# Long convolution plus top-128 experts: another order of GpSimd's work at the column loops, and another layout of the buffers there

## The chip, the cores and the metric

The kernel runs on one core of a Trainium2 chip. TensorE (PE in the profile), VectorE (DVE), ScalarE (ACT) and GpSimd (POOL) each run their own instruction list in order and meet at semaphores. SyncE (SP) issues nearly all DMAs, in order as well. The metric is device microseconds of one execution, the median of several; it is compared with the kernel before on the same chip.

## The reference

For 4 sequences of 12608 rows and 128 channels, in float32:

```
h_filt = (relu(pos_emb @ w1) @ w2) * exp(-0.01 * pos)
y = irfft(rfft(x * v, 2S) * rfft(h_filt, 2S), 2S)[:S]      # causal long convolution
x = x * y
# per sequence: the 128 rows with the highest score x @ w_gate get
out[row] = x[row] + sigmoid(score) * (relu(x[row] @ moe_w1) @ moe_w2)
```

All other rows of the output are x * y.

## The kernel before

The transforms are small matrix products. A sequence is laid out as a 111 x 115 grid, and the channels are worked in 32 groups of 4. There are 128 group steps t (4 sequences of 32), software-pipelined: step t does the inverse product of group t-3 (`f_i`, its result copied by ACT into `big`), the forward second product of group t (`dft`), the first product of group t+1 (`f_s1`), on DVE the spectrum product (`f_m`, `f_y`) of group t-1, on POOL the sums and differences of that spectrum (`f_sd` of t-1) and the product x * v for the input of group t+3 (`stage_u`). So POOL gets four operations a step, two of `f_sd` (L423, L424) and two of `stage_u` (L218, L219).

After the last group of a sequence, inside step 34, 66, 98 or 130, stands the column loop `P1.run` (L514). It finishes 116 columns in 29 turns h of four columns. Eight columns, two turns, make a block; there are 15 blocks. In a turn PE does the last small product (`mm`, L479 and L474), DVE multiplies it with x in place (`fin`, L489) and with the gate weights (L508), ACT sums the scores (L510), and after every second turn SP stores the block (L501) and loads x for the block five further on (L450). A load into a buffer waits until the store from that buffer has landed.

For blocks 2 to 14 POOL prepares, for four of the eight columns, the sum and the difference of two column planes (`comb`, L462); PE then needs half of the products for those columns and reads them at L474. Three such pairs of buffers are rotated (`cm`), and `comb` of three blocks is issued ahead of the loop.

At the three loops that are not the last, step 34 (66, 98) also completes the spectrum of its own group at once: line 959 runs `f_m`, `f_y` and `f_sd` of group 34 ahead of the loop, since the pipeline would otherwise hold the buffers through the loop.

All buffers are slices of one SBUF tile `arena`. Two of the six x buffers of the loop (XE) and the third `cm` pair (CE) are not slices of their own but lie over buffers of the group steps: `qs`, `mt`, `yz` and, behind these, `ws`, the scratch of the top-128 search. In words per partition these lie at: te 0, qs 1776, mt 2664, yz 3552 (two of 888), ws 5328 (640). CE is 1776 to 2800, the two XE 2800 to 3824 and 3824 to 4848. The loads into XE (blocks 4 and 5, issued ahead of the loop) therefore wait for all work on `mt` and `yz`. What may wait for what is worked out by the framework from these overlaps; the order on each engine is the order of the code.

Of the kernel before, what the change touches and what calls it, by code (L numbers as in the profile page):

```python
# [17 lines left out]
B, S, D, FO = 4, 12608, 128, 64  # L18
# [5 lines left out]
NG = 32  # L24
HC = 4 * N1
# [11 lines left out]
LAG = 3  # L37
# [4 lines left out]
NC, CO = 4, 2  # L42
# [5 lines left out]
CB = range(2, (NJ + 7) // 8)  # L48
PC = 4
OFF, _o = {}, 0  # L50
for _n, _k, _w in (("te", 2, 2 * HC), ("qs", 2, HC), ("mt", 1, 2 * HC), ("yz", 2, 2 * HC), ("ws", 1, 640), ("sd", LAG, 2 * HC),
                   ("ht", NH, 2 * HC), ("xa", NX, 8 * D), ("wx", 2, HB * D), ("cm", 2, 2 * NC * D), ("u", NU, 2 * XC)):
    OFF[_n] = (_o, _k, _w)
    _o += _k * _w
ARENA = _o
CE = OFF["qs"][0]
XE = [CE + 2 * NC * D + k * 8 * D for k in range(2)]
POS0, HID0 = 0, PJ * N1


# [80 lines left out]
def hyena_moe(ctx, tc, xg, x2, pos, bw, ww, wg, mw1, mw2, fo, c1, gx, cf, ci, wm, tk, zr, out):  # L141
    nc = tc.nc
# [6 lines left out]
    arena = cp.tile([128, ARENA], F32, name="arena")  # L149
    big = cp.tile([128, D * 2 * NJ], F32, name="big")  # L150

    def view(t, off, shape):
        n = int(np.prod(shape[1:]))
        r = t[:shape[0], off:off + n]
        if len(shape) > 2:
            ax = "abcd"[:len(shape) - 1]
            r = r.rearrange(f"p ({' '.join(ax)}) -> p {' '.join(ax)}", **dict(zip(ax[1:], shape[2:])))
        return r

    def buf(name, k, shape):  # L160
        o, n, w = OFF[name]
        return view(arena, o + k % n * w, shape)
# [40 lines left out]
    def rev(t):  # L203
        return t.rearrange("p (s i) -> p s i", i=N1)[:, :, ::-1]

    def nat(t):
        return t.rearrange("p (s i) -> p s i", i=N1)
# [6 lines left out]
    def stage_u(t):  # L214
        if t >= B * NG:
            return
        u = buf("u", t, [N1, 2, XC])
        nc.gpsimd.tensor_tensor(out=u[:, 0], in0=u[:, 0], in1=u[:, 1], op=ALU.mult)  # L218
        nc.gpsimd.tensor_tensor(out=u[:, 1].rearrange("p (s j) -> p s j", s=4),  # L219
                                in0=u[:, 0].rearrange("p (s j) -> p s j", s=4), in1=sg, op=ALU.mult)  # L220
# [186 lines left out]
    def f_m(t, uv):  # L407
        ht = buf("ht", t, [128, 2, HC])
        mt = buf("mt", t, [128, 2, HC])
        nc.vector.tensor_tensor(out=mt, in0=uv, in1=ht[:, 0].unsqueeze(1).to_broadcast([128, 2, HC]), op=ALU.mult)  # L410
        nc.vector.tensor_tensor(out=uv, in0=uv, in1=ht[:, 1].unsqueeze(1).to_broadcast([128, 2, HC]), op=ALU.mult)  # L411
        return mt

    def f_y(t, uv, mt):
        yz = buf("yz", t, [128, 2, HC])
        nc.vector.tensor_tensor(out=yz[:, 0], in0=uv[:, 1], in1=mt[:, 0], op=ALU.add)
        nc.vector.tensor_tensor(out=yz[:, 1], in0=mt[:, 1], in1=uv[:, 0], op=ALU.subtract)  # L417
        return yz

    def f_sd(t, yz):  # L420
        sd = buf("sd", t, [128, 2, HC])
        eng = nc.vector if t == B * NG - 1 else nc.gpsimd
        eng.tensor_tensor(out=nat(sd[:, 0]), in0=nat(yz[:, 0]), in1=rev(yz[:, 1]), op=ALU.add)  # L423
        eng.tensor_tensor(out=nat(sd[:, 1]), in0=rev(yz[:, 0]), in1=nat(yz[:, 1]), op=ALU.subtract)  # L424
        return sd.rearrange("p e (s i) -> p e s i", i=N1)
# [11 lines left out]
    class P1:  # L437
# [6 lines left out]
        def load_a(self, k):  # L444
            if k < len(blocks):
                j0, j1 = blocks[k]
                o = k % (NX + len(XE))
                self.xa[k] = buf("xa", o, [128, 8, D]) if o < NX else view(arena, XE[o - NX], [128, 8, D])
                for t in range(2):
                    nc.sync.dma_start(self.xa[k][t * NQ:t * NQ + PR, :j1 - j0], x2[self.b, t * PR:(t + 1) * PR, j0:j1])  # L450

        def comb(self, k):
            if k not in CB:
                return
            j0, j1 = blocks[k]
            j0 += CO
            n = min(NC, j1 - j0)
            o = (k - CB[0]) % 3
            cm = buf("cm", o, [128, 2, NC, D]) if o < 2 else view(arena, CE, [128, 2, NC, D])
            av = [ay[:, :, e * NJ + j0:e * NJ + j0 + n].rearrange("p g j s -> p j g s") for e in range(2)]  # L460
            for e, op in enumerate((ALU.add, ALU.subtract)):
                nc.gpsimd.tensor_tensor(out=cm[:, e, :n].rearrange("p j (g s) -> p j g s", s=4), in0=av[0], in1=av[1],  # L462
                                        op=op)
            self.cm[k] = cm

        def mm(self, h):
            ja, n = hbs[h]
            ps = self.s4[h] = ps1(h % 3, [128, HB, D], f"s4_{self.b}_{h}")
            for k in range(n - 1, -1, -1) if ja % 8 else range(n):
                j = ja + k  # L470
                a, c = CSH * j % N1, CSH * (N2 - j) % N1
                if j // 8 in CB and CO <= j % 8 < CO + NC:
                    for t, o in enumerate((a, c)):
                        nc.tensor.matmul(ps[t * NQ:(t + 1) * NQ, k], lhsT=gx_sb[:, o:o + NQ],  # L474
                                         rhs=self.cm[j // 8][:, t, j % 8 - CO], start=True, stop=True)
                    continue
                for e in range(2):
                    for t, o in enumerate((a, c + e * GW)):
                        nc.tensor.matmul(ps[t * NQ:(t + 1) * NQ, k], lhsT=gx_sb[:, o:o + NQ], rhs=ay[:, :, e * NJ + j],  # L479
                                         start=e == 0, stop=e == 1)  # L480

        def fin(self, h):
# [15 lines left out]
            if ja + n == blocks[blk][1]:  # L498
# [3 lines left out]
                if blk:  # L502
                    self.load_a(blk - 1 + NX + len(XE))

# [9 lines left out]
        def run(self, ex):  # L514
            self.wg = ps2(1, [128, D], f"wg_{self.b}")
            nc.scalar.copy(out=self.wg, in_=wgb)
            for k in range(len(XE)):
                self.load_a(NX + k)
            for k in range(3):
                self.comb(CB[0] + k)  # L520
            for h in range(len(hbs)):
                self.mm(h)
                self.fin(h)
                if h % 2 and h // 2 >= CB[0]:
                    self.comb(h // 2 + 3)
                if ex:
                    ex.hook(h, self.wg)
            nc.vector.tensor_tensor(out=self.sc, in0=self.sc, in1=negm, op=ALU.min)
            return self.sc
# [384 lines left out]
        nc.vector.memset(t, 0.0)  # L914
    h_hid()
    h_spec()
    te, uv, mt, sd, ph = {}, {}, {}, {}, {}
    bg = Background(iter(()))
    te[0] = f_s1(0)
    NT = B * NG  # L920
    for t in range(NT + LAG):
        g = t % NG
        i = t - LAG
        if 0 <= i:
            f_i(i, sd.pop(i))
        if t < NT:
            pq = ps2(1 - t % 2, [128, 2, 512], f"pq_{t}")
            spare[0] = [a[:, 512 - NS:] for a in bank1]
            uv[t] = pq[:, :, :HC]
            bg.now = t  # L930
            qs = dft(t, te.pop(t), (uv[t][:, 0], uv[t][:, 1]))
            bg.hook("p", 1)
            bg.hook("n", 1)
            if t + 1 < NT:
                te[t + 1] = f_s1(t + 1)
            spare[0] = None
            bg.hook("w", 1)
            load_u(t + NU - 1)
            if t == 8:
                for r in (PR, NQ + PR):  # L940
                    nc.sync.dma_start(arena[r:r + NQ - PR, OFF["xa"][0]:OFF["xa"][0] + NX * 8 * D], zr)
            o = t - 1 in uv
            if o:
                m = f_m(t - 1, uv[t - 1])
            f_v(uv[t], qs)
            for _ in range(ND):
                bg.hook("d")
            if o:
                y = f_y(t - 1, uv.pop(t - 1), m)
            f_u(uv[t], qs)  # L950
            if o:
                sd[t - 1] = f_sd(t - 1, y)
            stage_u(t + 3)
            if t:
                load_h(t + 2)
            for _ in range(NE):
                bg.hook("e")
            if i >= 0 and i % NG == NG - 1 or t == NT - 1:
                sd[t] = f_sd(t, f_y(t, uv[t], f_m(t, uv.pop(t))))
        if t >= NT:  # L960
            bg.now = t
            for _ in range((3, 1, 0)[t - NT]):
                bg.hook("p")
                for _ in range(ND):
                    bg.hook("d")
            bg.hook("w", 1)
        b = i // NG
        if i >= 0 and i % NG in LA:
            if i % NG == LA[0]:
                ph[b] = P1(b)  # L970
            ph[b].load_a(LA.index(i % NG))
        if i % NG == NG - 1 and i >= 0:
            bg.drain()
            ex = Experts(picked) if b + 1 == B else None
            sc = ph.pop(b).run(ex)
            bg = Background(topk_one(b, sc, ex))
# [50 lines left out]
```

## Time and profile before

| | us |
|---|---|
| median of 3 runs | 944.06 (943.54 to 945.16) |
| profiled execution, its own time | 944.23 |
| its span in the trace | 942.3 |
| PE busy | 902.8 (96%) |
| DVE busy | 854.4 (91%) |
| POOL busy | 769.3 (82%) |
| ACT busy | 613.3 (65%) |

PE's granted clock is 0.995 of full over the span. The span is the time from the first to the last instruction; 1.9 us of the execution's own time lie outside it. An engine's busy share is an average over three kinds of stretch: the filter's spectrum at the start, the group steps, and the column loops. The loops start at about 279, 473, 667 and 855 us of the span.

### The profile page before, as it was taken

What the parts mean: (1) busy time and instruction counts of PE and PEld (TensorE: products, weight loads), DVE (VectorE), ACT (ScalarE), POOL (GpSimd) and SP (SyncE); (2) the same over time, 40 slices, a digit from 0 to 9 for tenths busy, and PEclk for the clock granted to TensorE, in tenths of its full rate; (3) what the DMA queues carried; (4) which work ended last, traced back from release to release, by engine and by line L of the source; (5) the groups of instructions that cost most, each with busy time, mean ns of one, the idle gap of its engine ahead of it and who ended that gap; (6) DMA issues with size and microseconds to landing.
All of it is one profiled execution on the core that took longest, in us unless ns stands there. A gap on an engine that the chain in (4) does not pass through costs nothing.

```text
span 942.3 us, 37826 instructions
## 1 busy us (share of the span) xinstructions
PE 902.8 (96%) x15518; PEld 831.1 (88%) x15518; DVE 854.4 (91%) x1570; ACT 613.3 (65%) x1983; POOL 769.3 (82%) x714
## 2 busy tenths in 40 slices
PE   8999999999999999999999999999999999998964
PEld 5877789999999899999999999999999999988953
DVE  7999999999998899999988999999899999997974
ACT  5655545555547887865568878755599878545920
POOL 4898859999999579999998599999994999986701
PEclk9999999999999999999999999999999999999998
DMA  8144497666876886667958966669589666655830
GB/s 238 60 176 177 177 267 194 204 195 194 228 209 199 294 230 195 186 189 198 252 163 290 243 191 191 192 185 250 169 289 267 200 192 189 185 145 151 273 120 9
DMA packets 61408, 187.39 MB, mean 199 GB/s; under 512 B 8757, under 2 KB 12708, under 8 KB 61220
## 3 DMA queue, kind: packets, MB, share of 16 engines
q1 hardware_dynamic: 60980, 184.45, 65.1%
q8 instruction: 123, 2.02, 0.9%
q0 software_dynamic: 256, 0.52, 0.2%
q14 instruction: 49, 0.40, 0.1%
HBM read 143.52 MB, written 41.42 MB: 196 GB/s over the span
## 4 chain that ended last, share of the span: by engine, by line
PE 79%; DVE 6%; POOL 5%; DMA 4%; ACT 3%; issue 3%; SPq 0%; POOLq 0%; ACTq 0%; DVEq 0%
PE c L246 18%; PE c L230 10%; PE c L229 10%; PE a L230 10%; PE a L229 9%; PE a L479 5%; PE c L382 3%; PE a L362 3%; PE c L362 3%; PE c L479 3%; PE a L474 2%; ACT arena L510 2%; DMA out_dram<-arena 1%; POOL arena L423 1%; POOL arena L424 1%
## 5 line engine op out<-in xcount | busy, mean ns | idle before, releaser
L229 PE MATMUL c<-ci_sb,arena 128*56 128x116 f32 x2048 | 224.8, 263 | 4.3 <-POOL arena L423 2.0
L230 PE MATMUL c<-ci_sb,arena 128*55 128x116 f32 x2048 | 224.9, 263 | 0.0
L246 PE MATMUL c<-arena,cf_sb 128*64 128x222 f32 x2048 | 217.6, 351 | 2.2 <-DVE arena L417 1.9
L229 PE MATMUL a<-c_sb,arena 111*58 111x111 f32 x2048 | 217.0, 259 | 0.0
L230 PE MATMUL a<-c_sb,arena 111*57 111x111 f32 x2048 | 216.8, 259 | 0.0
L229 PEld LDWEIGHTS c<-ci_sb,arena 128*56 128x56 f32 x2048 | 206.5, 130 | 5.9 <-POOL arena L423 2.2
L230 PEld LDWEIGHTS c<-ci_sb,arena 128*55 128x55 f32 x2048 | 206.4, 129 | 0.0
L229 PEld LDWEIGHTS a<-c_sb,arena 111*58 111x58 f32 x2048 | 199.2, 132 | 4.3 <-issue 0.3
L230 PEld LDWEIGHTS a<-c_sb,arena 111*57 111x57 f32 x2048 | 199.0, 131 | 2.9
L423 POOL TENSOR_TENSOR arena<-arena 128x444 f32<-128x444 f32 x127 | 133.7, 1053 | 82.6 <-DVE arena L417 77.6
L246 PEld LDWEIGHTS c<-arena,cf_sb 128*64 128x64 f32 x2048 | 154.1, 137 | 27.6 <-ACT arena L238 2.3
L238 ACT COPY arena<-a 128x444 f32<-128x444 f32 x256 | 135.3, 530 | 63.6 <-PE a L230 63.2
L432 ACT COPY big<-c 128x928 f32<-128x928 f32 x128 | 118.3, 924 | 78.1 <-PE c L230 74.4
L510 ACT ACTIVATE arena<-arena 128x128 f32<-128x128 f32 x448 | 133.0, 298 | 27.4 <-DVE arena L508 25.2
L218 POOL TENSOR_TENSOR arena<-arena 111x460 f32<-111x460 f32 x128 | 150.2, 1174 | 0.0
L219 POOL TENSOR_TENSOR arena<-arena,wm_sb 111x460 f32<-111x460 f32 x128 | 139.4, 1089 | 10.0
L410 DVE TENSOR_TENSOR arena<-c,arena 128x888 f32<-128x888 f32 x128 | 138.4, 1081 | 3.8
L411 DVE TENSOR_TENSOR c<-c,arena 128x888 f32<-128x888 f32 x128 | 138.3, 1080 | 0.0
L424 POOL TENSOR_TENSOR arena<-arena 128x444 f32<-128x444 f32 x127 | 134.6, 1060 | 0.0
L462 POOL TENSOR_TENSOR arena<-big 128x512 f32<-128x512 f32 (+1 forms) x104 | 125.1, 1262 | 8.9 <-ACT big L432 5.6
L249 ACT COPY arena<-c 128x444 f32<-128x444 f32 x128 | 67.8, 529 | 58.6 <-PE c L246 55.2
L479 PE MATMUL a<-big,gx_sb 128*64 128x128 f32 x1472 | 100.6, 273 | 3.0 <-DVE arena L489 1.9
(188 smaller groups left out, 1675.8 us busy)
## 6 DMA issues: line engine op xcount, KB each, us to landing
arena<-hd SPq DMA_DIRECT2D x128, 444.0 KB
arena<-in_xg_dram SPq DMA_DIRECT2D x128, 402.5 KB
arena<-in_x_dram SPq DMA_DIRECT2D x112, 224.0 KB
out_dram<-arena SPq DMA_DIRECT2D x112, 224.0 KB
hd<-arena SPq DMA_DIRECT2D x32, 444.0 KB
arena<-in_pos_dram SPq DMA_DIRECT2D x14, 222.0 KB
arena<-in_moe_w_dram SPq DMA_DIRECT2D x2, 512.0 KB
arena<-in_x_dram SPq DMA_DIRECT2D x8, 112.0 KB
```

Of the source, the lines that this page charges most:

```text
L218: nc.gpsimd.tensor_tensor(out=u[:, 0], in0=u[:, 0], in1=u[:, 1], op=ALU.mult)
L219: nc.gpsimd.tensor_tensor(out=u[:, 1].rearrange("p (s j) -> p s j", s=4), in0=u[:, 0].rearrange("p (s j) -> p s j", s=4), in1=sg, op=ALU.mult)
L229: nc.tensor.matmul(o[:h], lhsT=lhsT[:, :h], rhs=rhs, **kw)
L230: nc.tensor.matmul(o[NQ:NQ + m - h], lhsT=lhsT[:, h:], rhs=rhs, **kw)
L238: nc.scalar.copy(out=te[:, e], in_=tps[e])
L246: nc.tensor.matmul(pq[w][e * NQ:(e + 1) * NQ, c], lhsT=cf_sb[:, 2 * w + e], rhs=te[:, e, c], start=True, stop=True)
L410: nc.vector.tensor_tensor(out=mt, in0=uv, in1=ht[:, 0].unsqueeze(1).to_broadcast([128, 2, HC]), op=ALU.mult)
L411: nc.vector.tensor_tensor(out=uv, in0=uv, in1=ht[:, 1].unsqueeze(1).to_broadcast([128, 2, HC]), op=ALU.mult)
L423: eng.tensor_tensor(out=nat(sd[:, 0]), in0=nat(yz[:, 0]), in1=rev(yz[:, 1]), op=ALU.add)
L424: eng.tensor_tensor(out=nat(sd[:, 1]), in0=rev(yz[:, 0]), in1=nat(yz[:, 1]), op=ALU.subtract)
L479: nc.tensor.matmul(ps[t * NQ:(t + 1) * NQ, k], lhsT=gx_sb[:, o:o + NQ], rhs=ay[:, :, e * NJ + j], start=e == 0, stop=e == 1)
L510: nc.scalar.activation(out=wx[:, k], in_=wx[:, k], func=AF.Copy, accum_out=self.sc[:, ja + k:ja + k + 1])
```

## The change

Three things move, and nothing is added or taken away in the count of operations.

At the loops inside steps 34, 66 and 98 `f_sd` of the step's own group is no longer issued ahead of the loop. `f_y` still is; its result stays in `yz` (`ys`), and `f_sd` runs one step later, where the ordinary pipeline has it. `stage_u` of group 37 (69, 101) is no longer issued ahead of the loop either, but in turn 23, behind the last `comb`.

The buffers are laid anew: the first XE lies at 1776 to 2800 (qs and the head of mt), the second at 4440 to 5464 (the second yz and the head of ws), and the two halves of the third `cm` pair at 2800 to 3312 (mt) and 5464 to 5976 (ws, which grows by 8 words). The first yz, which holds `ys` through the loop, is left free.

```
-XE = [CE + 2 * NC * D + k * 8 * D for k in range(2)]
+XE = [CE, OFF["yz"][0] + 2 * HC]
+CE = [XE[0] + 8 * D, XE[1] + 8 * D]
...
+                if h // 2 == CB[-1] - 3 and h % 2:
+                    stage_u((self.b + 1) * NG + 5)
...
-            if o:
-                sd[t - 1] = f_sd(t - 1, y)
-            stage_u(t + 3)
+            if o or t - 1 in ys:
+                sd[t - 1] = f_sd(t - 1, y if o else ys.pop(t - 1))
+            if i < 0 or i % NG < NG - 1:
+                stage_u(t + 3)
...
             if i >= 0 and i % NG == NG - 1 or t == NT - 1:
-                sd[t] = f_sd(t, f_y(t, uv[t], f_m(t, uv.pop(t))))
+                ys[t] = f_y(t, uv[t], f_m(t, uv.pop(t)))
+            if t == NT - 1:
+                sd[t] = f_sd(t, ys.pop(t))
```

In the rows of the order below, a bracket names the semaphores that an instruction waits for: an engine's, or one of the eight lanes DMAHW0 to DMAHW7 on which SP's DMAs land in turn. From `f_y` on the changed file's lines are one to four higher: `stage_u` is L219 and L220, `f_sd` L424 and L425, `comb` L464.

POOL at the first loop, from behind `f_sd` of group 33. Before:

```order
L218 TENSOR_TENSOR arena<-arena 111x460 [waits DMAHW3_49]
L219 TENSOR_TENSOR arena<-arena,wm_sb 111x460 [waits Pool_49]
L423 TENSOR_TENSOR arena<-arena 128x444 [waits DVE_49,PE_49]
L424 TENSOR_TENSOR arena<-arena 128x444 [waits PE_49]
L462 TENSOR_TENSOR arena<-big 128x512 [waits Activation_49]
L462 TENSOR_TENSOR arena<-big 128x512 x3
L462 TENSOR_TENSOR arena<-big 128x512 [waits Activation_49]
L462 TENSOR_TENSOR arena<-big 128x512
L462 TENSOR_TENSOR arena<-big 128x512 [waits PE_49,Pool_49] x18
L462 TENSOR_TENSOR arena<-big 128x256 [waits PE_49,Pool_49] x2
```

The same place on POOL in the changed kernel:

```order
L464 TENSOR_TENSOR arena<-big 128x512 [waits Activation_49]
L464 TENSOR_TENSOR arena<-big 128x512 x3
L464 TENSOR_TENSOR arena<-big 128x512 [waits DVE_49]
L464 TENSOR_TENSOR arena<-big 128x512
L464 TENSOR_TENSOR arena<-big 128x512 [waits PE_49,Pool_49] x18
L464 TENSOR_TENSOR arena<-big 128x256 [waits PE_49,Pool_49] x2
L219 TENSOR_TENSOR arena<-arena 111x460 [waits DMAHW3_49]
L220 TENSOR_TENSOR arena<-arena,wm_sb 111x460 [waits Pool_49]
L424 TENSOR_TENSOR arena<-arena 128x444
L425 TENSOR_TENSOR arena<-arena 128x444
```

The 26 `comb` operations now stand ahead of the four others, and the third pair waits for DVE.

SP at the same loop: the last load of a filter spectrum (`hd`), the four DMAs into the two XE (`in_x_dram`), and the stores of blocks 0 and 1. Before:

```order
L224 DMA arena<-hd 128x888 [waits DMAHW6_49,DVE_49]
L450 DMA arena<-in_x_dram 56x1024 [waits DMAHW7_49,DVE_49,Pool_49]
L450 DMA arena<-in_x_dram 56x1024 [waits DMAHW0_49]
L450 DMA arena<-in_x_dram 56x1024 [waits DMAHW1_49]
L450 DMA arena<-in_x_dram 56x1024 [waits DMAHW2_49]
L501 DMA out_dram<-arena 56x1024 [waits DMAHW3_49,DVE_49]
```

The same place on SP in the changed kernel:

```order
L225 DMA arena<-hd 128x888 [waits DMAHW6_49,DVE_49]
L451 DMA arena<-in_x_dram 56x1024 [waits DMAHW7_49,DVE_49,Activation_49]
L451 DMA arena<-in_x_dram 56x1024 [waits DMAHW0_49]
L451 DMA arena<-in_x_dram 56x1024 [waits DMAHW1_49,Pool_49]
L451 DMA arena<-in_x_dram 56x1024 [waits DMAHW2_49]
L503 DMA out_dram<-arena 56x1024 [waits DMAHW3_49,DVE_49]
```

The DMAs keep their order. The first load no longer waits for POOL; the third does. In the built program the values waited for name the instructions: before, DVE's L417 and POOL's L424 of group 34; in the changed kernel DVE's first operation of `f_y` of group 34 (L416 in the lines of before) and ACT's copy of `qs` of group 34 for the first load, and POOL's L424 of group 33 for the third.

DVE at the end of the first loop: the mask of the scores, then the start of the top-128 search, and the first operation of the next group step. Before:

```order
L528 TENSOR_TENSOR sc_2948<-sc_2948,tk_sb 128x116 [waits DVE_49,Activation_49]
L575 TENSOR_SCALAR f_4084<-sc_2948 128x116 [waits DVE_49]
L577 TENSOR_TENSOR sc_2948<-sc_2948,f_4084 128x116 [waits DVE_49]
L578 COPY hi_4085<-sc_2948 128x116 [waits DVE_49]
L650 CAST arena<-sc_2948 128x116
L405 TENSOR_TENSOR c_72<-c_72,arena 128x444 [waits Activation_49,Pool_49]
```

The same place on DVE in the changed kernel:

```order
L532 TENSOR_TENSOR sc_2948<-sc_2948,tk_sb 128x116 [waits DVE_49,Activation_49]
L579 TENSOR_SCALAR f_4082<-sc_2948 128x116 [waits DVE_49]
L581 TENSOR_TENSOR sc_2948<-sc_2948,f_4082 128x116 [waits DVE_49]
L582 COPY hi_4083<-sc_2948 128x116 [waits DVE_49]
L654 CAST arena<-sc_2948 128x116 [waits DMAHW4_49,DMAHW3_49]
L406 TENSOR_TENSOR c_72<-c_72,arena 128x444 [waits Activation_49]
```

The cast writes the head of `ws`, which now lies under the second XE, so it waits for the two lanes of the store of block 11, the last block in that buffer.

## Rows read from the trace of the kernel before

**Rows 1.** Groups by line: count | busy us, mean ns | idle before, by releaser.

```profile
L229 PE MATMUL c<-ci_sb,arena 128*56 128x116 f32 x2048 | 224.8, 263 | 4.3 <-POOL arena L423 2.0 <-DVE arena L423 0.8 <-ACT big L432 0.7
```

**Rows 2.** The waits: who waited for whom, us in total, times, longest.

```profile
PE a L474 <- POOL arena L462: 3.8, 6, 0.8
```

**Rows 3.** Timeline of PE, loop 1: start, us, engine, line, operation, count [idle before].

```profile
287.91 0.43 PE L474 MATMUL a<-arena,gx_sb 128*64 128x128 f32 x2 [0.42 <-POOL arena L462]
...
293.45 1.03 PE L479 MATMUL c<-big,gx_sb 128*64 128x128 f32 x14
...
297.38 1.03 PE L479 MATMUL c<-big,gx_sb 128*64 128x128 f32 x14
...
317.02 1.09 PE L479 MATMUL a<-big,gx_sb 128*64 128x128 f32 x16 [0.79 <-DVE arena L489]
...
322.33 0.26 PE L229 MATMUL c<-ci_sb,arena 128*56 128x116 f32 x1
```

**Rows 4.** Timeline of POOL, loop 1 and behind it.

```profile
282.27 1.16 POOL L218 TENSOR_TENSOR arena<-arena 111x460 f32<-111x460 f32 x1
...
285.57 1.06 POOL L424 TENSOR_TENSOR arena<-arena 128x444 f32<-128x444 f32 x1
286.58 31.21 POOL L462 TENSOR_TENSOR arena<-big 128x512 f32<-128x512 f32 x26
...
333.81 1.05 POOL L423 TENSOR_TENSOR arena<-arena 128x444 f32<-128x444 f32 x1 [13.73 <-DVE arena L417]
```

**Rows 5.** Timeline of SP's queue, loop 1: us is the time of issuing.

```profile
286.65 2.13 SPq L450 DMA_DIRECT2D arena<-in_x_dram  x4
288.89 3.15 SPq L501 DMA_DIRECT2D out_dram<-arena  x4
...
295.72 1.47 SPq L501 DMA_DIRECT2D out_dram<-arena  x2
...
320.57 7.86 SPq L501 DMA_DIRECT2D out_dram<-arena  x10
```

**Rows 6.** The waits of SP's queue, 275 to 300 us.

```profile
SPq L450 <- POOL arena L424: 2.6, 1, 2.6
```

**Rows 7.** Timeline of DVE, loop 1.

```profile
282.85 0.62 DVE L416 TENSOR_TENSOR arena<-c,arena 128x444 f32<-128x444 f32 x1
...
291.13 0.69 DVE L489 TENSOR_TENSOR arena<-c,arena 128x512 f32<-128x512 f32 x1
...
307.16 0.69 DVE L489 TENSOR_TENSOR arena<-a,arena 128x512 f32<-128x512 f32 x1 [1.64 <-DMA arena<-in_x_dram]
...
327.94 0.21 DVE L650 CAST arena<-sc 128x116 f32<-128x116 uint16 x1
```

**Rows 8.** Windows: busy by engine, then granted clock, DMA share, GB/s.

```profile
280.00:285.00 5.00, 5.00 (x92) 4.79 (x90) 4.86 (x8) 0.27 (x1) 4.68 (x5) 1.00 0.15 60
...
305.00:310.00 5.00, 5.00 (x94) 4.98 (x92) 3.32 (x6) 3.32 (x23) 5.00 (x5) 1.00 0.90 297
```

**Rows 9.** Timeline of PE, loops 2 and 3: first L474, first product behind the loop.

```profile
482.24 0.43 PE L474 MATMUL a<-arena,gx_sb 128*64 128x128 f32 x2 [0.57 <-POOL arena L462]
...
516.75 0.26 PE L229 MATMUL c<-ci_sb,arena 128*56 128x116 f32 x1
...
676.09 0.43 PE L474 MATMUL a<-arena,gx_sb 128*64 128x128 f32 x2 [0.43 <-POOL arena L462]
...
709.43 0.26 PE L229 MATMUL c<-ci_sb,arena 128*56 128x116 f32 x1
```

**Rows 10.** Timeline of DVE, loops 2 and 3: first operation of f_y.

```profile
477.04 0.62 DVE L416 TENSOR_TENSOR arena<-c,arena 128x444 f32<-128x444 f32 x1
...
671.02 0.62 DVE L416 TENSOR_TENSOR arena<-c,arena 128x444 f32<-128x444 f32 x1
```

**Rows 11.** Timeline of SP's queue, loops 2 and 3: the loads into XE.

```profile
481.00 1.84 SPq L450 DMA_DIRECT2D arena<-in_x_dram  x4
...
674.84 1.60 SPq L450 DMA_DIRECT2D arena<-in_x_dram  x4
```

More of the change, by code (lines that the diff above doesn't have):

```diff
@@ L50 @@
 OFF, _o = {}, 0
-for _n, _k, _w in (("te", 2, 2 * HC), ("qs", 2, HC), ("mt", 1, 2 * HC), ("yz", 2, 2 * HC), ("ws", 1, 640), ("sd", LAG, 2 * HC),
+for _n, _k, _w in (("te", 2, 2 * HC), ("qs", 2, HC), ("mt", 1, 2 * HC), ("yz", 2, 2 * HC), ("ws", 1, 648), ("sd", LAG, 2 * HC),
                    ("ht", NH, 2 * HC), ("xa", NX, 8 * D), ("wx", 2, HB * D), ("cm", 2, 2 * NC * D), ("u", NU, 2 * XC)):
@@ L458, in comb @@
             o = (k - CB[0]) % 3
-            cm = buf("cm", o, [128, 2, NC, D]) if o < 2 else view(arena, CE, [128, 2, NC, D])
+            cm = buf("cm", o, [128, 2, NC, D]) if o < 2 else None
+            cm = [view(arena, c, [128, NC, D]) if cm is None else cm[:, e] for e, c in enumerate(CE)]
             av = [ay[:, :, e * NJ + j0:e * NJ + j0 + n].rearrange("p g j s -> p j g s") for e in range(2)]
             for e, op in enumerate((ALU.add, ALU.subtract)):
-                nc.gpsimd.tensor_tensor(out=cm[:, e, :n].rearrange("p j (g s) -> p j g s", s=4), in0=av[0], in1=av[1],
+                nc.gpsimd.tensor_tensor(out=cm[e][:, :n].rearrange("p j (g s) -> p j g s", s=4), in0=av[0], in1=av[1],
                                         op=op)
@@ L474, in mm @@
                         nc.tensor.matmul(ps[t * NQ:(t + 1) * NQ, k], lhsT=gx_sb[:, o:o + NQ],
-                                         rhs=self.cm[j // 8][:, t, j % 8 - CO], start=True, stop=True)
+                                         rhs=self.cm[j // 8][t][:, j % 8 - CO], start=True, stop=True)
                     continue
@@ L916, in hyena_moe @@
     h_spec()
-    te, uv, mt, sd, ph = {}, {}, {}, {}, {}
+    te, uv, ys, sd, ph = {}, {}, {}, {}, {}
     bg = Background(iter(()))
```

## The prediction

> **What bounds the kernel now.** I read the page first: PE is busy for 902.8 of 942.3 us, so only its gaps can be won, and a slower engine matters where PE waits for it. The groups by line give PE's gaps at the step's products: a few us in all, 0.7 of them behind ACT's copy (L432), which stands just behind the column loops [rows 1]. The list of waits then names the gap that the change speaks of: PE at L474 waits for POOL's `comb`, six times, 3.8 us [rows 2]. Six is two in each of three loops; the fourth loop has none.
>
> The timelines of loop 1, one engine at a time, show why. PE comes to L474 at 287.49 (287.91 less 0.42 idle) [rows 3]. POOL starts its 26 `comb` operations only at 286.58, since it first runs `stage_u` of group 37 from 282.27 and `f_sd` of group 34 to 286.63 [rows 4]. That is the visible stall.
>
> The second thing stands on SP's queue. The loads of x for blocks 4 and 5 go out at 286.65 [rows 5], 0.02 us after POOL's L424 ends, and the queue's own waits say so: 2.6 us for that POOL operation, once [rows 6]. Everything behind them in the queue is late as well: the store of block 2 goes out at 295.72 [rows 5], though DVE finished turn 5, the block's last, at 291.82 (291.13 + 0.69) [rows 7]. In the window 280 to 285 the DMA engines are busy for 0.15 of the time, in 305 to 310 for 0.90 [rows 8]: the loop's DMA stream starts late and then runs close to full. DVE pays for it: at 307.16 it has been idle 1.64 us for x [rows 7], the first and longest of four such waits in loop 1 (3.75 us in all); and through DVE's result PE pays again, 0.79 us at 317.02 [rows 3].
>
> So in these loops two chains lie side by side, PE's products and SP's stream of x, and the later one sets the end.
>
> **The change part by part.** *The comb moved ahead.* POOL can start `comb` at 282.27 instead of 286.58 [rows 4]. The first pair (two operations; 31.21 us / 26 = 1.20 each) is ready by about 284.8, 2.7 us before PE's 287.49. The third pair waits for `f_y`, whose first operation ends at 283.47 [rows 7] and whose second follows directly (about 284.0); POOL reaches that pair at about 287. So PE's 3.8 us of stall go. Taken alone that is worth little: DVE would only arrive sooner at loads that come no sooner.
>
> *The new layout.* The first load then waits for the first operation of `f_y` (end 283.47, plus the 0.02 us of before: 283.49) and ACT's copy of `qs`, long done; the third for `f_sd` of group 33, done when POOL starts `stage_u` at 282.27. The stream of loop 1 starts 286.65 - 283.49 = 3.16 us earlier. In loops 2 and 3 `f_y`'s first operation ends at 477.66 and 671.64 [rows 10] and the loads go out at 481.00 and 674.84 [rows 11]: 3.32 and 3.18 us. The trace doesn't show how much of such a lead reaches the loop's end. From above it is all of it; from below nothing more than DVE's own lead, 1.2 us a loop, if stores wait for results. I take all of it, because the store of block 2 stands 3.9 us behind its result (295.72 against 291.82), more than the lead: the queue, not the result, is late from the start.
>
> *What PE can take.* Turns 8 and 11 start 293.45 and 297.38 [rows 3]: 3.93 us for three turns of 24 recorded products, 0.0546 us each. Behind the first L474 wait stand 25 turns less the 16 records of two full columns, 584 x 0.0546 = 31.89 us, less 0.22 because 287.49 is the end of a product and not its issue: 31.67. Measured from there to the first product behind the loop: 322.33 - 287.49 = 34.84 [rows 3]; 516.75 - 481.67 = 35.08 and 709.43 - 675.66 = 33.77 [rows 9]. PE's slack is thus 3.17, 3.41 and 2.10 us, POOL's stall included.
>
> *The smaller of lead and slack* is what a loop gives: 3.16 (loop 1), 3.32 (loop 2), 2.10 (loop 3), in sum 8.6 us. Behind the loops the group steps are PE-bound, so the lead stays. The waits for ACT's copy behind the loops, 0.7 us in all [rows 1], may shrink in loop 3; I count nothing.
>
> *The steps moved back.* `stage_u` of 37 and `f_sd` of 34 (1.05 to 1.16 us each by their rows, two and two) now run behind the last `comb`, with `stage_u` of 38 behind them: some 4.3 us more than POOL has there before. POOL is idle there for 13.73 us before the next `f_sd` [rows 4], and PE needs group 37's input and `f_sd` of 34 one and two steps later. Cost nothing; without that cover up to 4.3 us a loop.
>
> *The new waits at the loop's end.* DVE's cast at 327.94 [rows 7] waits for the store of block 11, ACT's copy of `qs` in step 35 for that of block 10. Before, DVE's `f_m` and `f_y` one step later waited for these stores. Behind the cast stands all of DVE, the next step's spectrum first. The last ten stores are issued from 320.57 to 328.43 [rows 5], 0.79 us each; block 11's two are the third and fourth, out by about 323.7. Since stores and DVE move by the same lead, I count nothing; the upper bound is a rival below.
>
> *Loop 4* has neither `f_sd` nor `stage_u` ahead of it: nothing changes.
>
> The 0.90 of the window 305 to 310 [rows 8] bears on the lead. The Trainium skill ("DMA: Bandwidth & Descriptors", section "Why a DMA increments its semaphore by 16 and not by 1") says that a DMA runs on the largest number of engines, at most 16, that divides both sides' outer size; for 56 rows that would be 14, a busy share of 0.875. By that rule the stream is full from the middle of the loop, cannot close up, and no more than the lead can be won: 9.7 us over three loops, 934.6 at best; if the share were no ceiling, the stream could shorten, and PE's slack alone (8.7 us) and the waits behind the loops would limit, 934.9. The trace agrees with the rule (0.90, with the little traffic of other queues).
>
> **The sum.** The profiled execution took 944.23 us (942.3 span, 1.9 outside, unchanged), 0.17 above the median of 944.06. 944.23 - 8.6 = 935.6.
>
> **The rivals.**
>
> *A. The lead is lost on the way.* Stores must wait for DVE's results, and those come only as much earlier as POOL's stall is long. Then only rows 2's 3.8 us are won: 940.4. For it: the store of block 1 needs turn 3's result, which doesn't move. Against: the 3.9 us by which the queue trails.
>
> *B. No change.* PE's stall goes and comes back as DVE's wait for x, because the loads in fact start when they did, held by something ahead of them in SP's queue. In loops 1 and 2, DVE's waits for x exceed POOL's stall, so all would be given back: 944.2. Against: the queue's wait ended with POOL's L424 to 0.02 us [rows 4, 5], and the new order asks no longer for that operation.
>
> *C. Slower.* The cast behind the store of block 11. DVE is in order, so it stands still until the store lands, and the next step's spectrum with it. Each us that the store lands after DVE's arrival costs one a loop; it outweighs the gain when it passes 8.6 / 3 = 2.9 us. At 4 us: 944.2 + 3 x 1.1 = 947.6. For it: block 11's stores are out only some 4 us before the cast's time now, and the stream is near full. Against: loads and stores move forward with DVE, and the wait is for a store that another four blocks' stores follow.
>
> **How the numbers follow.** Forecast 0.66, A 0.20, B 0.08, C 0.06. The likeliest time is 935.6; its own range is 934.0 (all PE slack, 8.7, the 0.7 behind the loops, and as much again for gaps too short for the trace) to 938 (a lead that arrives by two thirds). With A the range reaches to 941. This kernel's times can be told apart from 0.2%, 1.9 us: faster holds forecast and A, 0.86; same is B, 0.08; slower is C, 0.06.
>
> **What would show it.** Right: no wait of PE at L474 for POOL; the loads for blocks 4 and 5 issued within 0.1 us of `f_y`'s first operation, 3.2 us earlier against PE's first product of the loop; in loop 1 the stretch from L474 to the next step near 31.7 us; DVE still waiting for x in the second half of loops 1 and 2, but for less; POOL's moved operations ended long before the next `f_sd`. Wrong: loads that start no sooner; a DVE wait of over 1 us at the cast, or of ACT at `qs`; PE waiting for POOL in the steps behind a loop.

## The result, and the profile after

The changed kernel took 935.85 us (median of 6 runs, 932.32 to 937.3) against 943.85 (6 runs, 942.26 to 947.21) for the kernel before on the same chip: a ratio of 0.9908, 95% interval 0.9894 to 0.9921. Forecast were 935.6. The profiled execution took 936.24 us, its span is 934.2 (before 942.3), PE's mean granted clock 0.989 of full (before 0.995); over each of loops 1 to 3 it is 1.00 in both, so the loops are compared at the same clock.

To see where the 8.1 us of span came from, cut PE's timeline at each loop's first product and at the first product behind the loop. Before, loop 1 runs from 279.22 to 322.33.

| us | before | after | gain |
|---|---|---|---|
| up to loop 1 | 279.22 | 278.71 | 0.51 |
| loops 1, 2, 3 | 43.11, 43.34, 41.85 | 39.98, 40.38, 39.98 | 3.13, 2.96, 1.87 |
| steps behind loops 1, 2, 3 | 151.07, 150.64, 145.40 | 151.39, 150.49, 145.70 | -0.32, 0.15, -0.30 |
| loop 4 | 39.89 | 39.89 | 0 |
| behind loop 4 | 47.80 | 47.71 | 0.09 |

The three loops give 7.96 of the 8.1. The following rows answer to those shown of before. First PE in loop 1 (start, us, engine, line, operation, count, idle before), as in [rows 3]:

```profile
286.82 0.61 PE L476 MATMUL a<-arena,gx_sb 128*64 128x128 f32 x8
...
318.26 0.61 PE L476 MATMUL a<-arena,gx_sb 128*64 128x128 f32 x8
318.70 0.26 PE L230 MATMUL c<-ci_sb,arena 128*56 128x116 f32 x1
...
324.09 0.31 PE L230 MATMUL c<-ci_sb,arena 128*56 128x116 f32 x1 [0.61 <-ACT big L433]
```

No row of the loop has an idle time. From the first product that reads `comb` to the first behind the loop are 318.70 - 286.82 = 31.88 us, PE's own pace: before, those from 287.91 to 322.33 took 34.42 [rows 3]. The wait of PE for `comb` [rows 2] is gone from the list of waits, and so is PE's for POOL in the groups by line:

```profile
L476 PE MATMUL a<-arena,gx_sb 128*64 128x128 f32 x544 | 41.3, 273 | 0.0
```

POOL, as in [rows 4]:

```profile
281.76 20.10 POOL L464 TENSOR_TENSOR arena<-big 128x512 f32<-128x512 f32 x16
302.27 11.44 POOL L464 TENSOR_TENSOR arena<-big 128x512 f32<-128x512 f32 x10 [0.41 <-PE a L476]
313.67 1.17 POOL L219 TENSOR_TENSOR arena<-arena 111x460 f32<-111x460 f32 x1
...
319.24 1.08 POOL L220 TENSOR_TENSOR arena<-arena,wm_sb 111x460 f32<-111x460 f32 x1
330.17 1.05 POOL L424 TENSOR_TENSOR arena<-arena 128x444 f32<-128x444 f32 x1 [9.85 <-DMA arena<-hd]
```

`comb` starts directly behind `f_sd` of group 33; the moved operations, with `stage_u` of group 38 behind them, end at 320.32, and POOL is still idle 9.85 us before the next `f_sd` (13.73 before).

SP's queue in loop 1, as in [rows 5], then its waits from 275 to 300 us (waiting line, releaser: us, times, longest), as in [rows 6]:

```profile
283.03 1.61 SPq L451 DMA_DIRECT2D arena<-in_x_dram  x4
284.74 3.58 SPq L503 DMA_DIRECT2D out_dram<-arena  x4
...
317.00 7.71 SPq L503 DMA_DIRECT2D out_dram<-arena  x10
```

```profile
SPq L451 <- DVE arena L417: 5.0, 1, 5.0
```

The loads go out 4.32 us behind the loop's first product, not 7.43, and the queue now waits for `f_y` in place of POOL's `f_sd`. From the first load's issue to the start of the run of ten stores are 33.97 us, before 33.92 [rows 5]: the stream begins earlier and keeps its length. DVE, as in [rows 7]:

```profile
282.35 0.62 DVE L417 TENSOR_TENSOR arena<-c,arena 128x444 f32<-128x444 f32 x1
...
306.06 0.69 DVE L491 TENSOR_TENSOR arena<-a,arena 128x512 f32<-128x512 f32 x1 [0.24 <-DMA arena<-in_x_dram]
...
312.59 0.69 DVE L491 TENSOR_TENSOR arena<-a,arena 128x512 f32<-128x512 f32 x1 [1.50 <-PE c L476]
...
318.26 0.69 DVE L491 TENSOR_TENSOR arena<-c,arena 128x512 f32<-128x512 f32 x1 [0.80 <-DMA arena<-in_x_dram]
...
324.34 0.21 DVE L654 CAST arena<-sc 128x116 f32<-128x116 uint16 x1
```

DVE still waits for x, but in loop 1 for 0.24 + 1.50 + 0.80 = 2.54 us, not 3.75. (The 1.50 names PE, which was busy throughout and ahead; as the same operation has no wait where x comes in time, I read it as a load too. The 3.75 of before hold a wait of 1.15 us that names PE in the same way.) The cast has no idle time before it. The same windows as in [rows 8] (the last two columns are the share of the DMA engines and GB/s):

```profile
280.00:285.00 5.00, 5.00 (x94) 4.78 (x91) 4.86 (x8) 0.27 (x1) 5.00 (x5) 1.00 0.25 74
305.00:310.00 5.00, 5.00 (x97) 5.00 (x94) 4.68 (x9) 4.62 (x31) 4.91 (x5) 1.00 0.87 275
```

PE and SP in loops 2 and 3, as in [rows 9] and [rows 11]:

```profile
507.80 1.10 PE L481 MATMUL a<-big,gx_sb 128*64 128x128 f32 x16 [0.18 <-DVE arena L491]
...
510.47 0.26 PE L230 MATMUL c<-ci_sb,arena 128*56 128x116 f32 x1
...
700.95 0.26 PE L230 MATMUL c<-ci_sb,arena 128*56 128x116 f32 x1
```

```profile
474.42 1.91 SPq L451 DMA_DIRECT2D arena<-in_x_dram  x4
```

```profile
665.28 1.79 SPq L451 DMA_DIRECT2D arena<-in_x_dram  x4
```

Loop 2 is the only one where PE still waits: 0.18 us for DVE, which had itself waited 1.63 us for x.

Loop 4 shows in both kernels what a loop with neither chain late takes. In the kernel before, the loads into its two XE go out 3.81 us ahead of its first product (at 854.64), PE has no wait for `comb` there, and it lasts 39.89 us:

```profile
850.83 1.89 SPq L450 DMA_DIRECT2D arena<-in_x_dram  x4
```

### The profile page after: what moved, and what is told of

Its sections match the earlier page's. It is cut to its first block, busy times and chain, and to the rows that moved or that the text cites. A ratio compares the mean times of both kernels' runs of the same rounds, so it can differ in the third digit from the quotient of the medians.

```text
span 934.2 us, 37841 instructions
## 1 busy us (share of the span) xinstructions
PE 903.1 (97%) x15518; PEld 829.0 (89%) x15518; DVE 854.4 (91%) x1570; ACT 612.7 (66%) x1983; POOL 769.7 (82%) x714
## 3 DMA queue, kind: packets, MB, share of 16 engines
q8 instruction: 123, 2.02, 0.9%
## 4 chain that ended last, share of the span: by engine, by line
PE 81%; DMA 8%; DVE 5%; issue 2%; POOL 2%; ACT 1%; SPq 1%; POOLq 0%; DVEq 0%; ACTq 0%
PE c L247 19%; PE c L230 12%; PE a L230 10%; PE a L231 10%; PE c L231 10%; PE a L481 5%; DMA out_dram<-arena 3%; PE c L383 3%; PE a L363 3%; PE c L363 3%; DMA arena<-in_x_dram 3%; PE c L481 2%; PE a L476 2%; DVE ms L601 1%; PE a L310 1%
## 5 line engine op out<-in xcount | busy, mean ns | idle before, releaser
L231 PE MATMUL c<-ci_sb,arena 128*55 128x116 f32 x2048 | 226.1, 264 | 0.0
L231 PE MATMUL a<-c_sb,arena 111*57 111x111 f32 x2048 | 216.8, 259 | 0.0
L231 PEld LDWEIGHTS c<-ci_sb,arena 128*55 128x55 f32 x2048 | 207.7, 130 | 0.0
L231 PEld LDWEIGHTS a<-c_sb,arena 111*57 111x57 f32 x2048 | 199.0, 131 | 2.8
L424 POOL TENSOR_TENSOR arena<-arena 128x444 f32<-128x444 f32 x127 | 133.7, 1053 | 71.7 <-DVE arena L418 45.5
L247 PEld LDWEIGHTS c<-arena,cf_sb 128*64 128x64 f32 x2048 | 149.6, 137 | 31.4 <-ACT arena L239 2.3
L219 POOL TENSOR_TENSOR arena<-arena 111x460 f32<-111x460 f32 x128 | 149.9, 1171 | 1.0 <-DMA arena<-in_xg_dram 1.0
L220 POOL TENSOR_TENSOR arena<-arena,wm_sb 111x460 f32<-111x460 f32 x128 | 139.3, 1088 | 10.0
L464 POOL TENSOR_TENSOR arena<-big 128x512 f32<-128x512 f32 (+1 forms) x104 | 125.7, 1247 | 11.0 <-ACT big L433 6.2
L425 POOL TENSOR_TENSOR arena<-arena 128x444 f32<-128x444 f32 x127 | 134.5, 1059 | 0.0
L406 DVE TENSOR_TENSOR c<-c,arena 128x444 f32<-128x444 f32 x128 | 80.2, 627 | 15.8 <-ACT arena L250 15.7
```

What stands on the lines that cost most here:

```text
L231: nc.tensor.matmul(o[NQ:NQ + m - h], lhsT=lhsT[:, h:], rhs=rhs, **kw)
L247: nc.tensor.matmul(pq[w][e * NQ:(e + 1) * NQ, c], lhsT=cf_sb[:, 2 * w + e], rhs=te[:, e, c], start=True, stop=True)
L464: nc.gpsimd.tensor_tensor(out=cm[e][:, :n].rearrange("p j (g s) -> p j g s", s=4), in0=av[0], in1=av[1], op=op)
```

## The experiments

The theory is the prediction's: two chains lie side by side in a column loop, PE's products and SP's stream of loads and stores, and the later one ends it. It needs both parts of the change. Rival A says that the stall of PE behind `comb` is all that is won. So the two parts were pulled apart. This table holds what each profiled run shows: the issue of the first XE load behind the loop's first product, loops 1 to 3, and the steps behind them. Ratios are to the kernel before, run on the same chip (medians 944.71 us for the first four kernels, 945.0 for the next four, 945.81 for the last three).

| kernel | `comb` ahead | load at | loops | steps behind | median | ratio, 95% |
|---|---|---|---|---|---|---|
| before | no | 7.4 to 7.6 | 43.11, 43.34, 41.85 | 151.07, 150.64, 145.40 | | 1 |
| e_late | yes | 6.9 to 7.1 | 40.68, 41.51, 42.34 | 151.39, 150.84, 145.76 | 943.12 | 0.9993, 0.9976 to 1.0009 |
| e_half | yes | 5.6 to 5.9 | 40.49, 40.16, 40.43 | 151.70, 150.65, 146.90 | 937.99 | 0.9933, 0.9902 to 0.9965 |
| e_layout | no | 4.3 | 41.82, 42.04, 41.86 | 150.25, 150.23, 145.35 | 937.95 | 0.9941, 0.9914 to 0.9968 |
| e_stage_ahead | yes | 4.3 | 39.98, 40.08, 39.98 | 152.31, 150.26, 145.11 | 936.36 | 0.993, 0.9904 to 0.9956 |
| e_late0 | yes | 8.2 | 41.14, 42.97, 43.33 | 153.95, 150.84, 147.00 | 947.33 | 1.0019, 1.0002 to 1.0036 |
| e_swap | yes | 3.1 to 3.3 | 39.98, 39.98, 39.98 | 150.56, 150.28, 145.83 | 935.22 | 0.99, 0.9878 to 0.9923 |
| e_layout_again | no | 4.3 | 41.82, 42.01, 41.86 | 150.26, 150.24, 145.81 | 940.18 | 0.9947, 0.9924 to 0.9969 |
| e_moe_early | yes | 4.3 | 39.99, 40.88, 39.98 | 152.66, 150.53, 145.91 | 937.77 | 0.9917, 0.989 to 0.9945 |
| e_after_again | yes | 4.3 | 39.99, 39.98, 40.00 | 152.69, 150.28, 146.62 | 936.26 | 0.9894, 0.9865 to 0.9922 |
| e_swap_again | yes | 3.1 to 3.3 | 39.98, 39.98, 39.98 | 150.58, 150.27, 145.42 | 933.62 | 0.9875, 0.9847 to 0.9903 |
| e_swap_moe | yes | 3.1 to 3.3 | 39.98, 39.98, 39.98 | 150.57, 150.27, 145.82 | 936.09 | 0.9901, 0.9874 to 0.9929 |

### The order alone: `comb` ahead, but the loads late (e_late, e_late0, e_half)

```
-        def comb(self, k):
+        def comb(self, k, hold=None):
...
+                if hold == (k, e):
+                    nc.gpsimd.memset(view(arena, XE[0], [128, 1]), 0.0)
...
+            for k in range(3):
+                self.comb(CB[0] + k, HOLD if self.b + 1 < B else None)
             for k in range(len(XE)):
                 self.load_a(NX + k)
-            for k in range(3):
-                self.comb(CB[0] + k)
```

The loads of blocks 4 and 5 must follow the memset, a POOL operation of 0.13 us; `HOLD` sets behind which `comb` operation it stands: the second, (2, 1), in e_half, the third, (3, 0), in e_late, and the fourth, (3, 1), in e_late0 (the fourth operation, not the fourth pair as the expectation has it). The new layout stays, so these kernels hold everything of the change but the early loads.

> The changed kernel, but ahead of the loads for blocks 4 and 5 POOL writes one zero column into the first XE buffer behind the third comb operation (loops 1 to 3), so that these loads start some 6.9 us behind the loop's first product: 0.5 us sooner than in the kernel before, 2.6 us later than in the changed kernel. POOL's comb stays first, so PE does not wait at L474. Theory (a loop gives the smaller of the stream's lead and PE's slack): 0.5 us a loop, about 942.4 against 943.9 before, DVE waiting over 3 us for x in loops 1 and 2. Rival A (only POOL's stall counts): 3.8 us won, 940.1. If the layout's lead did nothing at all: as the changed kernel, 935.9.

> As the run before, but the column is written behind the second comb operation: the loads start some 5.7 us behind the loop's first product, a lead of 1.8 us over the kernel before, about half of the changed kernel's. Theory: 1.8 us a loop in all three (loop 3's slack is 1.9), 5.3 in sum, about 938.6; loops of some 41.4, 41.6 and 40.1 us from the first product to the next step's. Rival A: 940.1, and the same as with the loads still later.

> The changed kernel with one more instruction: POOL clears a column of the first XE behind the 4th pair of comb operations, so that the loads of blocks 4 and 5 go out about 8.1 us behind PE's first product of the loop, 0.7 later than in the kernel before, while comb stays ahead and PE has no stall for POOL at the start of the loop. Theory (the later of SP's stream and PE's products sets the loop's end): nothing is left of the gain, the three loops last 42.3 to 43.8 us each, 944 to 945.5. Rival A (the gain is POOL's stall taken from PE): 940.1, loops of about 41.5 to 42.

With the loads back near their old place nothing is left of the gain: 0.9993 and 1.0019, though PE no longer waits for `comb` in either. A forecast 940.1, a gain of 3.8 us; by the ratios e_late is 0.7 us faster than the kernel before (at most 2.3 by the interval) and e_late0 1.8 us slower, which refutes it. In e_late0 POOL, SP and the waits of 280 to 327 us show what took the stall's place:

```profile
282.07 5.04 POOL L465 TENSOR_TENSOR arena<-big 128x512 f32<-128x512 f32 x4
287.02 0.13 POOL L468 MEMSET arena<- 128x1 f32 x1
```

```profile
287.18 1.60 SPq L452 DMA_DIRECT2D arena<-in_x_dram  x4
```

```profile
DVE arena L494 <- DMA arena<-in_x_dram: 5.4, 7, 1.9
...
PE c L231 <- ACT big L434: 0.9, 1, 0.9
PE a L231 <- DVE arena L494: 0.7, 1, 0.7
PE a L484 <- DVE arena L494: 0.6, 1, 0.6
```

PE, free of its stall, runs ahead, DVE waits 5.4 us for x, and PE then waits for DVE. Two of the three PE waits (L231) lie behind the loop: part of the lateness leaves the loop and shows in the steps, 153.95 us against 151.07 in the kernel before. That is why loop 1 was shorter than forecast (41.14 us, not 42.3 or more) and the time longer: 1.8 us over the kernel before on its chip, 2.3 by the medians, where the forecast meant 0.15 to 1.65 over its 943.85. With half of the lead, e_half gained most of it: 937.99, forecast 938.6.

The medians of e_late and e_half came as the theory has them; their single loops did not. At 0.5 us a loop e_late's would take 42.6, 42.8 and 41.3 us. They took 40.68, 41.51 and 42.34, in sum 3.8 less than before, which is A's figure; the steps gave 0.9 back, and that execution, 940.4 us, lies 2.7 under the kernel's median. For e_half 41.4, 41.6 and 40.1 were forecast, and 40.49, 40.16 and 40.43 came, with 2.1 us lost in the steps. So the rule of the smaller part does not tell a single loop of these kernels to better than some 2 us, and the case against A rests on the medians.

### The layout alone: the loads early, PE's stall left (e_layout, e_layout_again)

```
-                if h // 2 == CB[-1] - 3 and h % 2:
-                    stage_u((self.b + 1) * NG + 5)
...
-            if o or t - 1 in ys:
-                sd[t - 1] = f_sd(t - 1, y if o else ys.pop(t - 1))
-            if i < 0 or i % NG < NG - 1:
-                stage_u(t + 3)
+            if o:
+                sd[t - 1] = f_sd(t - 1, y)
+            stage_u(t + 3)
...
-                ys[t] = f_y(t, uv[t], f_m(t, uv.pop(t)))
...
+                sd[t] = f_sd(t, f_y(t, uv[t], f_m(t, uv.pop(t))))
```

> The new layout alone: stage_u of 37 and f_sd of 34 stand ahead of comb as in the kernel before, the loads for blocks 4 and 5 start as early as in the changed kernel. Theory: PE waits again 1.2 to 1.4 us a loop for POOL at L474, and that time is lost, since with the lead the loop runs at PE's pace behind it: loops of some 41.2 us, gains of about 1.9, 2.0 and 0.7, 4.5 in sum, about 939.4. If only the stream counted: 935.9. If only the stall counted: 943.9.

> The new layout alone once more, stage_u and f_sd ahead of comb as before, with more rounds. Theory as corrected after the first try (a stall of PE ahead of comb's product costs more than its visible gap): loops of 41.8 to 42.0 us, 1.8 to 2.0 over the changed kernel's, so 3 x 1.87 = 5.6 us above the changed kernel: 941.4. The first try's median, 937.95, would be 2.1 above it; if that comes again, the loops' loss is made up elsewhere, in the stretch behind the fourth loop.

The loads go out as in the changed kernel (SP) and PE waits as before (PE, loop 1):

```profile
283.10 1.62 SPq L451 DMA_DIRECT2D arena<-in_x_dram  x4
```

```profile
287.47 0.43 PE L476 MATMUL a<-arena,gx_sb 128*64 128x128 f32 x2 [0.42 <-POOL arena L464]
288.69 0.54 PE L476 MATMUL a<-arena,gx_sb 128*64 128x128 f32 x5 [0.78 <-POOL arena L464]
```

The two profiled runs agree to 0.03 us in each loop, and in loop 1 DVE has no wait for x any more: PE ends these loops, at 39.98 plus its stall. The stall costs 1.84, 2.06 and 1.88 us, more than the visible 1.20 that my 41.2 went by, so loop 3 wins nothing here and the other two 1.3 each. By the ratios the kernel is 5.6 and 5.0 us faster than before; loops and steps in the two profiled runs account for 3.9 and 3.4 (575.41 us in sum before, 571.55 and 572.00 here). In those two executions the stretch behind the fourth loop was 2.7 and 1.4 us shorter than before as well; it differs that much between executions of one kernel (below), so that the layout wins anything there is not shown. The rough sum of the two ways, 0 to 1 for the order and 5 to 6 for the layout, is less than the 8.0 of both. By the medians each part is worth more with the other; the intervals (the layout alone 3 to 8 us) leave it open.

### `stage_u` ahead, `f_sd` behind (e_stage_ahead)

```
-                if h // 2 == CB[-1] - 3 and h % 2:
-                    stage_u((self.b + 1) * NG + 5)
...
-            if i < 0 or i % NG < NG - 1:
-                stage_u(t + 3)
+            stage_u(t + 3)
```

> The changed kernel with stage_u of 37 back ahead of comb (f_sd of 34 stays behind it). POOL then starts comb 2.3 us later, at about 5.3 us behind the loop's first product; the first pair is ready at about 7.8, and PE comes for it at 8.1. Theory: as the changed kernel, 935.9, no wait of PE at L474, since one of the two moves is enough. Otherwise the pair is late by up to 0.5 us a loop: 937.4.

```profile
281.21 1.18 POOL L219 TENSOR_TENSOR arena<-arena 111x460 f32<-111x460 f32 x1
282.47 1.09 POOL L220 TENSOR_TENSOR arena<-arena,wm_sb 111x460 f32<-111x460 f32 x1
283.51 2.56 POOL L464 TENSOR_TENSOR arena<-big 128x512 f32<-128x512 f32 x2
```

`comb` starts 5.35 us behind PE's first product (3.05 in the changed kernel), its first pair ends at 286.07, and PE, which comes there at 286.27 (8.11 behind its first product at 278.16), does not wait. The loops are the changed kernel's. On POOL, moving `f_sd` alone was enough.

### An earlier stream still (e_swap, e_swap_again, e_after_again)

```
-XE = [CE, OFF["yz"][0] + 2 * HC]
-CE = [XE[0] + 8 * D, XE[1] + 8 * D]
+XE = [OFF["yz"][0] + 2 * HC, CE]
+CE = [XE[1] + 8 * D, XE[0] + 8 * D]
```

> The changed kernel with the two XE changed round, so that the loads of block 4 wait only for f_sd of group 33 and can go out some 1.2 us earlier than in the changed kernel; those of block 5 still wait for f_y. Theory (in the changed kernel PE's own products set the end of loops 1 and 3, 39.98 us each): loops 1 and 3 stay at 39.98, loop 2 comes to between 40.0 and 40.4, and the time is within 0.5 us of the changed kernel's, 935.5 to 936.2. Rival (the stream still sets the end): each loop gains up to 1.2 us more, 932.3.

> The two XE changed round, a second time, beside the changed kernel on the same chip. Theory: all three loops at 39.98, so 0 to 0.4 us in loop 2 below the changed kernel and up to 0.6 in ACT's copy behind loop 1 (0.61 us of idle in the changed kernel, none here): 0 to 1.0 below it, not told apart. Rival (starting the stream earlier still pays in full): 2 to 3.6 us below it.

> The changed kernel, unaltered, beside the next two. Theory: loops 1 and 3 at 39.98 us, loop 2 between 39.98 and 40.4, 934.5 to 936.5.

In e_swap_again SP's queue starts 3.12 us behind PE's first product, and waits for `f_sd` of group 33 first:

```profile
281.58 1.96 SPq L451 DMA_DIRECT2D arena<-in_x_dram  x4
```

```profile
SPq L451 <- POOL arena L425: 2.2, 1, 2.2
```

All three loops now last 39.98 us: PE's products end them and an earlier stream can't shorten them, as the theory had it. But something was left behind the loops. The changed kernel, run again, shows it in PE's timeline behind loop 1:

```profile
323.81 0.30 PE L230 MATMUL a<-c_sb,arena 111*58 111x111 f32 x1 [0.75 <-DVE arena L491]
325.66 0.31 PE L230 MATMUL c<-ci_sb,arena 128*56 128x116 f32 x1 [0.87 <-ACT big L433]
```

In both runs of e_swap neither row has an idle time, and the steps behind loop 1 take 150.6 us, against 151.39 and 152.69 in the changed kernel's two profiled runs. So the changed kernel's stream is still a little late at the end. Whether the swap beats it in time is not settled: 935.22 and 933.62 us against 935.85 and 936.26; over 12 runs each the means are 934.7 and 935.9, and the spread of single runs is 5 us for one and 7 us for the other. Side by side on one chip, e_swap_again is 2.6 us below the changed kernel, more than the 0 to 1.0 that I had forecast and within the rival's 2 to 3.6. The rival's way to it, shorter loops, is refuted (39.98 in all); in the two profiles the steps are 3.3 us shorter, 2.1 of them behind loop 1 and 1.2 behind loop 3. An earlier stream pays there and not in the loops, as far as two executions show it.

### The expert weights (e_moe_early, e_swap_moe)

Behind loop 4 the traces last between 45.0 and 49.2 us. In the changed kernel PE waits there for the two loads of the expert weights, which SP issues behind turns 22 and 25:

```profile
889.76 0.44 PE L230 MATMUL a<-arena 128*64 128x128 f32 x1 [2.68 <-DMA arena<-in_moe_w_dram]
...
895.09 0.29 PE L230 MATMUL c<-arena 128*64 128x128 f32 x1 [1.95 <-DMA arena<-in_moe_w_dram]
```

The edits, in the changed kernel and in e_swap:

```
-MW = 22
+MW = 0     # e_moe_early;  e_swap_moe: 12
```

> The changed kernel with the two loads of the expert weights issued in turns 0 and 3 of the fourth column loop, not in turns 22 and 25. In the traces so far the stretch behind the fourth loop lasts 45.0 us where these weights land in time and 47.7 to 48.0 where PE waits for them. Theory: 45.0 us each time, so 936 - 2.7 = 933.2. Rival: the weights delay the loop's loads and stores of x, the fourth loop becomes longer than 39.89 by what the tail gains, 935 to 936.5; or the tail's length has another cause (the clock), and nothing changes.

> The two XE changed round, and the expert weights loaded in turns 12 and 15 of the fourth loop, not in 22 and 25. Theory: the weights land ahead of the tail (45.0 us in place of 45.8 to 47.7), and if the fourth loop's stream has 2 us of room by turn 12, the loop stays at 39.89: 0.8 to 2.7 below the kernel with the two XE changed round alone. Rival (there is no room in that stream, as with the loads in turns 0 and 3, where the loop grew by 1.4 and the tail did not shrink): the same time or up to 2 us longer.

The waits for the weights went, and nothing was won: 937.77 and 936.09. Loop 4 grew from 39.89 to 41.27 and 40.62, and the stretch behind it was 48.35 and 46.98. Idle times of PE in e_moe_early:

```profile
887.13 1.09 PE L481 MATMUL a<-big,gx_sb 128*64 128x128 f32 x16 [0.73 <-DVE arena L491]
890.33 0.55 PE L851 MATMUL c<-ident,xe 128*128 128x128 f32 x3 [0.35 <-DVE arena L491]
894.96 0.47 PE L230 MATMUL a<-arena 128*64 128x128 f32 x1 [4.08 <-ACT arena L852]
```

The weights pushed back x, so DVE came late and PE behind it; and in place of the weights PE then waits 4.08 us for ACT's copy of the picked rows (L852). The rival held in both: the fourth loop grew, and the stretch behind it did not shrink to 45.0. That stretch's length explains part of what single runs differ by: it was 45.1 and 46.4 us in the two profiled runs of the layout alone, 47.8 before. What sets it is open. PE's granted clock there does not order it: 45.1 us at 0.82 (e_layout), 47.8 at 0.89 (before), 49.2 at 0.79 (e_late0).

## Why the prediction was right, point by point

**The order.** Right: no wait of PE for `comb`, and without the early loads worth nothing that can be told from noise (e_late, e_late0).

**The new layout and the lead.** The loads start 3.11, 3.27 and 3.13 us earlier against PE's first product (7.43, 7.60, 7.45 less 4.32, 4.33, 4.32); forecast were 3.16, 3.32 and 3.18. That they were held by POOL's `f_sd` and by nothing else is shown, so B fell.

**How much of the lead arrives.** This was chosen, not read: all of it. Loop 1 bears it out, where the stream kept its length (33.97 us, before 33.92). That length is no constant: with the loads at 4.3 us it took 31.9 to 34.7 us in loops 1 to 3 of the traces, so one loop shows the arrival to a us or so. The three kernels with `comb` ahead and a later stream show it in time, which falls with the lead (loads at 8.2, 7.0, 5.7 and, in the changed kernel, 4.3 us: 1.0019, 0.9993, 0.9933, 0.9908).

**What PE can take.** The pace of 0.0546 us gave 31.89 us from the first product that reads `comb` to the next step; measured 31.88. PE's floor for a loop is 39.98 and e_swap reaches it three times.

**The smaller of the two.** Loop 1: 3.13, forecast 3.16. Loop 2: 2.96, forecast 3.32; 0.40 us of x late were left in that execution, and none in the changed kernel's second profile (39.98). Loop 3: 1.87, forecast 2.10. Here I had misread a row: the first product behind loop 3 stands at 709.23 in the trace, and 709.43 [rows 9] is a later one of the same form, so the slack was 1.90. The sum was 7.96 in place of 8.6. That the time came within 0.3 us of the forecast is in part luck: the loops gave 0.6 us less than the sum had, and the kernel before took 943.85, 0.4 less than the 944.23 that the sum starts from. The 0.51 us up to loop 1, where nothing was changed, are no gain: that stretch lasts 278.2 to 279.7 us over all traces.

**The steps moved back.** Nothing, as forecast: 9.85 us of POOL's idle time remain.

**The new waits at the loop's end.** None at the cast (324.34 directly follows 324.20 + 0.22), so C fell.

**Behind the loops.** Counted at nothing, with a remark that ACT's copy might give 0.7. This term was mis-sized: in the first profile the steps lost 0.47, in the second 0.87 + 0.75 us of idle time stand behind loop 1, and e_swap shows some 0.8 to 2.1 us to be had there. The prediction asked when PE's products end; DVE, ACT and the stores still work on the last blocks then, and the next step needs their result.

**The share of the DMA engines.** In the eight windows of 5 us from 285 to 325 it is at most 0.90 in before, the changed kernel, e_late0, e_layout and e_swap_again, and 0.91 in e_half and e_swap. The Trainium skill ("DMA: Bandwidth & Descriptors", section "Why a DMA increments its semaphore by 16 and not by 1") makes 56 rows run on 14 of 16 engines, 0.875; the traces agree with it to the traffic of other queues. They also hold the semaphore steps of each DMA. For the first load into XE in loop 1 of the changed kernel one step comes 0.49 us behind the issue and 14 more between 2.35 and 3.03; all 240 loads and stores of x have that number, while a load of `hd` (128 rows) has 16, that of `c_sb` (111 rows) one early and 3, and one of 8 rows one early and 8. That the stream "cannot close up" went too far: with its late start in e_late0 it took 38.2 us in loop 1 from the first load to the last store's start, 40.9 before and 41.1 in the changed kernel.

## What to carry to other kernels

Where two chains run side by side through a stretch, measure the length of each, and its start: a change is worth the smaller of what it gives to the later chain and the room to the other, and mending one visible stall alone can be worth nothing. Look for what the queue's first transfer waits for; the 3 us there, at the head of a nearly full stream, arrived at its end here. Then see whether the next stretch starts from the engine that you followed or from one that trails it.

## What the runs showed of the hardware that was not expected

The idle time shown before a product understates what a stall costs. In e_layout, 0.42 + 0.78 = 1.20 us stand before products of loop 1, and the loop is 1.84 longer than PE's pace (loops 2 and 3: 1.42 for 2.06, 1.23 for 1.88). The start times account for the difference. The second wait is for the difference plane, which POOL finishes one `comb` operation later than the sum. The product that reads it starts 9.91 us behind the loop's first product (288.69 less 278.78). In the changed kernel, where nothing waits, products start in pairs 0.007 us apart, a pair every 0.109 us, and this one starts at 8.11, just behind the first that reads the sum (286.82 less 278.71). It is thus 1.80 us late (2.02 and 1.83 in loops 2 and 3), nearly all of the loss. Of the 1.80 the idle time leaves out the 0.43 us between the two gaps, in which the two records that wait for the sum alone run, and about 0.17 in which earlier records still run ahead of the first gap.

One execution is not the kernel: e_late's profiled run, 940.4 us, was the lowest of its ten (up to 945.56), e_late0's, 949.32, the highest of its twelve (from 944.71). What a profile tells of a single us counts only where it comes twice or where the medians agree.
